# Two mab stages and a gated feed-forward on one Trainium2 core: earlier loads and transposes for the second batch, two dummy matmuls, one matmul fewer

## The chip, the cores and the metric

The kernel runs on one core of one Trainium2 chip. The core has a matrix engine (PE, with its weight loads shown apart as PEld), a vector engine (DVE), a scalar engine (ACT), a general engine (POOL) and a queue engine (SP). Each of them works through its own list of instructions in order; semaphores tie them together. DMA transfers are issued from the lists of SP and POOL and run beside them. The metric is the device time of one execution in microseconds.

## The reference

```python
def _attn_ref(x, inducing):                     # x: 4 x 12416 x 128, inducing: 32 x 128
    def mab(q, kv):
        s = scale * (q @ kv.transpose(0, 2, 1))
        s = s - s.max(-1, keepdims=True)
        a = np.exp(s)
        a /= a.sum(-1, keepdims=True) + 1e-09
        return a @ kv
    h = mab(I, x)                               # I: inducing for each of the 4 batches
    return mab(x, h)

def _moe_ref(x, w_gate, w_val, w_out):          # d_model 128, d_ff 1536
    gate = 1.0 / (1.0 + np.exp(-(x @ w_gate)))
    val = x @ w_val
    return gate * val @ w_out
```

For each batch, 32 inducing rows attend to all 12416 tokens and give `h` (stage 1). Every token then attends to the 32 rows of its batch's `h` (stage 2), and the result goes through a gated feed-forward.

## The kernel before, in words

A batch's 12416 tokens are 97 chunks of 128. They are handled in seven groups: six of 16 chunks and one of a single chunk (group 6). A group's tokens are loaded once into `xn` (`x_load`, issued from POOL's list) and are needed transposed in `xT`.

Stage 1 of a group: `s1_score` multiplies `xT` with the scaled inducing rows (L210) and DVE takes the negated maximum (`nm`, L222); `s1_exp` gives the exponentials `a1T` on ACT (L235); they are turned into `a1`, on PE with a copy (L248, L254) or by a DMA transpose (L259); `s1_sum` multiplies them with `xn` (L270). When all groups are through, their partial sums are brought to one maximum and added: that is `h` in transposed form, `hT`. Stage 2 of a group: scores of `xT` with `hT` (L443), maximum, exponential, sum and scaling, partly on POOL (L490 to L558). The attention weights `a2n` are turned by a DMA transpose from SP's list into `a2r` (L569).

The feed-forward doesn't use the attention output itself: `hw` holds the products of `h` with both weight matrices (L341), and 32 rows of `a2r` times 32 rows of `hw` give the two hidden halves at once (L850). The main loop runs over 97 blocks of four chunks; a block's 12 hidden chunks are eight steps `t`, alternately of two chunks and of one. A step is: `hidden_mm` for the value half and, two steps ahead, for the gate half on PE, tanh on ACT (`t`, L869), and the product `u = (t + 1) * v` on DVE (L882), which takes 776 steps with two of them cut in half. Two steps later `project` multiplies `u` with `w_out` on PE (L913).

Two steps are a slot. All other work of the loop is put beside the steps by a hand-written table: `at(slot, make)` records what is to be emitted behind the even step of a slot, or with `late=True` behind the odd one. What is emitted in a slot stands at that place in every engine's list, so a waiting instruction holds back what stands behind it on its engine. While the batch `b` is in the loop, the table holds stage 1 of batch `b + 1` (`plan_stage1`: score, exponential one slot later, turn two slots later, sums in the slots that are given) and stage 2 of both. `x_transpose_dma` issues one group's DMA transpose from `xn` to `xT` on SP (L90). PSUM tiles are named by tags; `m` is the one bank for all work of the table.

Before the loop stands a prologue for the first batch, for which nothing can be hidden: its groups are turned on PE (L637), and its last groups `sa`, `sb`, `sc` end with the chain that this change touches. The maxima of all groups are joined (`ml`, L708; L712, L713; `top`, L715), the weights `wl` are formed on ACT (L735), the four parts `hw_parts` are multiplied with them (POOL L737, ACT L738 and L748, DVE L750), and `h_add` adds them up by a matmul each (L756); `h_take` scales the sum to `hT` (L335). `keep_on(n, tag)` issues `n` matmuls of 128 x 512 whose result nobody reads (`w_ps`, L103).

Of the second batch's tokens two groups are loaded in the prologue and four in slot 3. Their transposes stand in the slots of this line, group by group:

```python
when = 3 * g if b else (9, 11, 14, 17, 20, 23, 12)[g]
```

Of the kernel before, what the change touches and what calls it, by code (L numbers as in the profile page):

```python
# [13 lines left out]
ALU = mybir.AluOpType  # L14
# [11 lines left out]
def kernel(  # L26
# [9 lines left out]
    nc = tc.nc  # L36
# [6 lines left out]
    NG = NCH // GC  # L43
# [29 lines left out]
    def x_load(b, s, first=0):  # L73
        c0, n = groups[s]
        if s == 0:
            c0, n = 0, n + NLO
        if b not in xn:
            xn[b] = xnp.tile([P, NCH, C], F16, tag="xn", name=f"xn_{b}")
        cuts = [c0, c0 + first, c0 + n] if first else [c0, c0 + n]
        for c, e in zip(cuts, cuts[1:]):  # L80
            nc.gpsimd.dma_start(xn[b][:, c:e, :], xv[b, :, c:e, :])  # L81
# [5 lines left out]
    def x_transpose_dma(b, s):  # L87
        c0, n = groups[s]
        xT_tile(b)
        nc.sync.dma_start(  # L90
            xT[b][:, c0 : c0 + n, :],
            xn[b][:, c0 : c0 + n, :].rearrange("p j c -> p (j c)"),
            transpose=True,
        )
# [5 lines left out]
    def keep_on(n, tag):  # L100
        w_ps = ps.tile([P, 4, P], F32, tag=tag, name="w_ps")
        for _ in range(n):
            nc.tensor.matmul(w_ps[:], idle[:, 0, :], idle, start=True, stop=True)  # L103
# [11 lines left out]
        out=identf[:],  # L115
# [18 lines left out]
        wo16[:].rearrange("p (q i) c -> p q (i c)", i=NI // 2),  # L134
        moe_w_out.rearrange("(q p i) c -> p q (i c)", p=P, i=NI // 2),
    )
    for g in range(2):
        x_load(1, g)

    ident = const.tile([P, P], F16, tag="ident")  # L140
# [42 lines left out]
    def s1_sum(b, s, a1, tag):  # L183
        hp = ps.tile([P, C + 1], F32, tag=tag, name="hp_ps")
        s1_sum_pe(b, s, a1, hp, 0, 4)
        return s1_sum_keep(b, s, hp)
# [3 lines left out]
    def at(slot, make, late=False):  # L190
        plan.setdefault((slot, late), []).append(make)
# [8 lines left out]
    def s1_dims(s):  # L200
        n = groups[s][1]
        ng = min(4, n)
        return ng, n // ng, 32 * ng
# [40 lines left out]
    def s1_turn_pe(b, s, a1T, tag="m"):  # L244
        ng, w, R = s1_dims(s)
        aT = ps.tile([P, 4, P], F16, tag=tag, name="aT_ps")
        for k in range(w):
            nc.tensor.transpose(aT[:, k, 0:R], a1T[0:R, ts(k, P)], ident[0:R, 0:R])  # L248
        return aT

    def s1_turn_copy(s, aT, copy=nc.vector.tensor_copy):
        ng, w, R = s1_dims(s)
        a1 = s1p.tile([P, 4, P], F16, tag="a1")
        copy(out=a1[:, 0:w, 0:R], in_=aT[:, 0:w, 0:R])  # L254
        return a1
# [31 lines left out]
    def plan_stage1(b, s, score, total):  # L287
        st = {}
        full = groups[s][1] == GC

        def begin():
            st["s1"] = s1_score(b, s, "m")

        def weigh():
            st["a1T"] = s1_exp(b, s, st["s1"])

        def turn():
            if full:
                st["a1"] = s1_turn_dma(b, s, st["a1T"])
            else:  # L300
                st["a1"] = s1_turn_copy(s, s1_turn_pe(b, s, st["a1T"]))

        at(score, begin)
        at(score + 1, weigh, late=full)
        at(score + 2, turn)
        first, second, keep = total

        def part(k0, k1):
            if k0 == 0:
                st["hp"] = ps.tile([P, C + 1], F32, tag="m", name="hp_ps")  # L310
            s1_sum_pe(b, s, st["a1"], st["hp"], k0, k1)

        at(first, lambda: part(0, 2))
        at(second, lambda: part(2, 4))
        at(keep, lambda: s1_sum_keep(b, s, st["hp"]))
# [12 lines left out]
    def l_inverse(l_ps):  # L328
        li = bp.tile([P, m], F32, tag="li")
        nc.vector.reciprocal(out=li[:], in_=l_ps)  # L330
        return li

    def h_take(b, h_ps, li):
        hT16[b] = bp.tile([P, m], F16, tag="hT", name="hT")
        nc.vector.tensor_tensor(out=hT16[b][:], in0=h_ps, in1=li[:], op=ALU.mult)  # L335
# [308 lines left out]
    a1T, a1 = {}, {}  # L644
    nm1, l1, hst = nm1s[0], l1s, hsts[0]
    for p in range(-2, NS - 3):
# [5 lines left out]
        if p >= 0:  # L652
            s = arrival[p]
            aT = s1_turn_pe(0, s, a1T[s])
# [5 lines left out]
        if p == EARLY - 2:  # L660
            we = const.tile([P, EARLY], F32, tag="we")
            nc.vector.tensor_reduce(
                out=nml[:, 0:1], in_=nm1[:, 0:EARLY], axis=AX.X, op=ALU.min
            )
            nc.scalar.activation(
                out=we[:], in_=nm1[:, 0:EARLY], func=AF.Exp, bias=nml[:, 0:1], scale=-1.0
# [19 lines left out]
    sc, sb, sa = arrival[-1], arrival[-2], arrival[-3]  # L686
# [4 lines left out]
    for j0, tag, copy in ((GC // 2, "v2", nc.scalar.copy), (GC - BC, "g1", nc.vector.tensor_copy)):  # L691
# [15 lines left out]
    ml = const.tile([P, 1], F32, tag="ml")  # L707
    nc.vector.tensor_reduce(out=ml[:], in_=nml[:], axis=AX.X, op=ALU.min)  # L708
    a1[sa] = s1_turn_copy(sa, s1_turn_pe(0, sa, a1T[sa]))
    low_ps = ps.tile([P, 2, 512], F32, tag="v2", name="low_ps")  # L710
    mlT_ps, arg_ps = low_ps[0:1, 0, 0:P], low_ps[:, 1, 0:NL]
    nc.tensor.matmul(arg_ps, identf[:], nml[:], start=True, stop=True, skip_group_check=True)  # L712
# [3 lines left out]
        out=top[:],  # L716
# [2 lines left out]
        op=ALU.min,  # L719
        negate=True,  # L720
    )
    a1[sb] = s1_turn_copy(sb, s1_turn_pe(0, sb, a1T[sb], "g2"), nc.scalar.copy)
    hps = [s1_sum(0, sa, a1[sa], "acc")]
    a1[sc] = s1_turn_copy(sc, s1_turn_pe(0, sc, a1T[sc], "v1"))
    for g in range(4):
# [8 lines left out]
    wl = const.tile([P, NL], F32, tag="wl")  # L734
    nc.scalar.activation(out=wl[:], in_=arg_ps, func=AF.Exp, scale=-1.0)  # L735
    hw_parts = [hpart[0][:]] + [hst[:, NS - k, 0:C] for k in range(1, NL)]
# [8 lines left out]
        out=e32l[:], in0=e32[:], scalar1=lsum[:], scalar2=TINY, op0=ALU.mult, op1=ALU.add  # L745
# [1 line left out]
    hps.append(s1_sum(0, sb, a1[sb], "m"))  # L747
    nc.scalar.mul(out=hw_parts[2], in_=hps[1], mul=wl[:, 2:3])  # L748
    hps.append(s1_sum(0, sc, a1[sc], "g1"))
    nc.vector.tensor_scalar_mul(out=hw_parts[3], in0=hps[2], scalar1=wl[:, 3:4])  # L750

    h_ps = ps.tile([P, m], F32, tag="g2", name="h_ps")
    l_ps = ps.tile([P, m], F32, tag="v2", name="l_ps")
# [1 line left out]
    def h_add(k, first=False, last=False):  # L755
        nc.tensor.matmul(h_ps[:], hw_parts[k], e32[:], start=first, stop=last)  # L756
# [1 line left out]
    h_add(1, first=True)  # L758
    nc.tensor.matmul(l_ps[:], ones[:], e32l[:], start=True, stop=True)
    h_add(0)  # L760
    h_add(2)
    h_add(3, last=True)
    h_take(0, h_ps[:], l_inverse(l_ps[:]))


    s2_a = ps.tile([P, GC, m], F32, tag="m", name="s2_ps")
# [4 lines left out]
        out=nmx_a[:], in_=s2_a[:, 0:BC, :], axis=AX.X, op=ALU.max, negate=True  # L771
# [3 lines left out]
        out=low[:],  # L775
        in0=s2_a[:, 0:BC, :],
        in1=nmx_a[:].unsqueeze(2).to_broadcast((P, BC, m)),
# [6 lines left out]
    for hf, tag in enumerate(("g1", "v1")):  # L784
# [7 lines left out]
        out=a2n_a[:],  # L792
        in0=e_a[:],
        in1=rs_a.unsqueeze(2).to_broadcast((P, BC, m)),
# [144 lines left out]
    for b in range(B):  # L939
        o = base[b]  # L940
        more = b + 1 < B

        if b == 0:
            plan_stage2(0, groups[1][0], o, None, o + 3, soon=True)
            plan_stage2(0, groups[2][0], o + 5, o + 7, o + 18)
        for s in range(3 if b == 0 else 2, NG - 1):
            k = o + 16 * s - 28
            plan_stage2(b, groups[s][0], k, k + 2, k + (14 if more else 10))
        plan_stage2(b, groups[NG - 1][0], o + 56, o + 58, o + 66, far=o + 52)
        if not more:  # L950
            continue
        early = (
            [(13, (18, 19, 19)), (16, (23, 23, 23))]
            if b == 0
            else [(8, (15, 16, 17)), (12, (18, 19, 19))]
        )
        later = [(24, (31, 31, 31)), (28, (35, 35, 35)), (40, (47, 48, 49)), (44, (50, 51, 51))]
        for s, (score, total) in enumerate(early + later + [(32, (43, 43, 43))]):
            plan_stage1(b + 1, s, o + score, [o + e for e in total])
        plan_combine(b + 1, o + 52, o + 55, [(o + 72, o + 74), (o + 80, o + 82)])  # L960
        plan_stage2(b + 1, groups[0][0], o + 67, o + 70, o + 78)
        plan_stage2(b + 1, groups[1][0], o + 84, o + 86, o + 94)
        for g in range(NS):
            when = 3 * g if b else (9, 11, 14, 17, 20, 23, 12)[g]
            at(o + when, lambda b=b, g=g: x_transpose_dma(b + 1, g))
            if b == 0 and 2 <= g < NG:
                at(o + 3, lambda g=g: x_load(1, g))
        if b + 2 < B:
            for g in range(NG):
                at(o + (28 if b == 0 else 24, 33, 42, 60, 60, 82)[g], lambda b=b, g=g: x_load(b + 2, g))  # L970
# [56 lines left out]
```

## Time and profile before

| what | value |
|---|---|
| time, median of 3 runs | 729.22 us (726.39, 729.22, 729.37) |
| the profiled execution's own time | 729.32 us |
| its span, first to last instruction | 727.5 us |
| mean granted clock of PE | 0.993 |
| first product `u` on DVE | 32.32 us from the span's start |
| HBM read and written | 27.80 MB and 25.43 MB |

All places in time are microseconds from the start of the span. In a row of the timeline stand the start, the duration (for several instructions from the first to the end of the last), the engine, the line, the operation with output and inputs, the count, and in brackets the engine's idle time ahead of it with what ended it. Rows of stretches give the busy time of each engine, with the number of instructions in brackets. The time of a run lies 1.82 us over the span of the profiled one.

### The profile page before, as it was taken

How to read it: one execution, taken by the hardware profiler on the slowest of the kernel's cores; microseconds unless marked ns; L12 is line 12 of the kernel's file. 1: busy time of each engine (PE TensorE's matmuls, PEld its weight loads, DVE VectorE, ACT ScalarE, POOL GpSimd, SP SyncE). 2: the span in 40 equal slices, each digit the busy share in tenths (PEclk: the TensorE clock that was granted, in tenths of full speed). 3: DMA queues.
4: the chain of work that ended last, by engine and by line, in shares of the span. 5: the costliest groups of instructions: out<-in, count | busy, mean ns of one | idle time of the engine just before them, and what ended most of it. 6: DMA issues, size and time to landing. Idle time of an engine off the chain costs nothing.

```text
span 727.5 us, 21568 instructions
## 1 busy us (share of the span) xinstructions
PE 649.0 (89%) x8478; PEld 392.9 (54%) x8478; DVE 704.4 (97%) x871; ACT 674.6 (93%) x1008; POOL 420.4 (58%) x699
## 2 busy tenths in 40 slices
PE   7888898999998988999988989999989899898887
PEld 4554555555555555555555545555555555555555
DVE  4798999999999999999999999999999999999998
ACT  4697999999999999999999999999999999999996
POOL 4471846788764548488757275387865665636200
PEclk9998999999999999999999999999999999999999
DMA  9797755154558272326188540330332121121211
GB/s 173 138 197 152 127 113 102 48 108 82 73 119 174 62 148 68 81 64 126 50 114 163 103 89 31 88 69 36 76 59 74 46 59 58 54 66 45 61 45 46
DMA packets 116726, 65.21 MB, mean 90 GB/s; under 512 B 99824, under 2 KB 101008, under 8 KB 116624
## 3 DMA queue, kind: packets, MB, share of 16 engines
q1 hardware_dynamic: 111936, 49.81, 31.1%
q0 software_dynamic: 4416, 13.90, 10.7%
q8 instruction: 66, 1.08, 0.6%
q14 instruction: 36, 0.29, 0.2%
q10 hardware_dynamic: 272, 0.13, 0.1%
HBM read 27.80 MB, written 25.43 MB: 73 GB/s over the span
## 4 chain that ended last, share of the span: by engine, by line
DVE 50%; issue 21%; PE 16%; ACT 9%; DMA 3%; DVEq 1%; POOL 0%; ACTq 0%; POOLq 0%
DVE u L882 48%; ACT t L869 8%; PE acc_ps L913 7%; PE v_ps L850 6%; DMA xn<-in_x_dram 2%; DVE nm L222 2%; DMA xT<-xn 1%; DVEq L882 1%; PE hp_ps L270 1%; PE g_ps L850 1%; POOL xn L81 0%; PE w_ps L103 0%; PE s_ps L443 0%; ACT hwt L351 0%; PE s_ps L210 0%
## 5 line engine op out<-in xcount | busy, mean ns | idle before, releaser
L882 DVE SCALAR_TENSOR_TENSOR u<-t,v_ps 128x512 f16<-128x512 f16 (+1 forms) x778 | 675.7, 945 | 3.8 <-PE g_ps L850 2.7
L869 ACT ACTIVATE t<-g_ps 128x512 f16<-128x512 f32 (+1 forms) x777 | 593.6, 818 | 32.3 <-ACT t L869 17.0
L850 PE MATMUL v_ps<-a2r,hwt 32*128 32x512 f16 (+1 forms) x1188 | 294.1, 372 | 65.3 <-DVE u L882 64.4
L913 PE MATMUL acc_ps<-wo,u 128*128 128x128 f16 x4656 | 329.0, 221 | 0.0
L913 PEld LDWEIGHTS <-u 128*128 128x128 f16 x4656 | 262.4, 98 | 89.2 <-issue 88.1
L850 PE MATMUL g_ps<-a2r,hwt 32*128 32x512 f16 (+1 forms) x1188 | 297.2, 379 | 0.0
L850 PEld LDWEIGHTS <-hwt 32*128 32x128 f16 x2424 | 91.0, 91 | 197.1 <-issue 152.2
L512 POOL TENSOR_TENSOR sum<-e 128x256 f32<-128x256 f16 (+1 forms) x23 | 15.5, 672 | 146.7 <-ACT e L504 145.2
L558 POOL TENSOR_TENSOR a2n<-e,rs 128x2048 f16<-128x2048 f16 (+3 forms) x25 | 86.8, 3475 | 5.6 <-DVE rs L530 2.4
L536 POOL TENSOR_TENSOR near<-sme,minus 128x16 f32<-128x16 f32 (+1 forms) x22 | 65.2, 2965 | 1.8
L931 ACT ACTIVATE o<-acc_ps 128x512 f32<-128x512 f32 x96 | 58.1, 605 | 0.0
L491 POOL TENSOR_SCALAR rise<-rise 128x256 f32<-128x256 f32 (+6 forms) x110 | 51.2, 466 | 9.7
L490 POOL TENSOR_TENSOR rise<-sc 128x256 f32<-128x256 f32 (+1 forms) x22 | 16.2, 738 | 38.6 <-ACT sc L480 38.4
L492 POOL TENSOR_TENSOR top<-top,rise 128x128 f32<-128x128 f32 (+3 forms) x88 | 28.4, 323 | 7.3
L512 POOL TENSOR_TENSOR sum<-sum 128x128 f32<-128x128 f32 (+3 forms) x92 | 28.4, 309 | 7.2
L490 POOL TENSOR_TENSOR rise<-top 128x128 f32<-128x128 f32 (+3 forms) x88 | 27.3, 311 | 6.9
L495 POOL TENSOR_TENSOR sc<-sc,top 128x512 f32<-128x512 f32 (+1 forms) x22 | 23.9, 1086 | 1.7
L443 PEld LDWEIGHTS <-xT 128*128 128x128 f16 x388 | 13.2, 96 | 11.7 <-issue 11.7
L443 PE MATMUL s_ps<-hT,xT 128*128 128x32 f16 x388 | 18.1, 178 | 0.3 <-DVE hT L335 0.3
L222 DVE TENSOR_REDUCE nm<-s_ps 128x1 f32<-128x512 f32 (+1 forms) x25 | 15.5, 618 | 2.3 <-PE s_ps L210 2.3
L235 ACT ACTIVATE a1T<-s_ps,nm 128x512 f16<-128x512 f32 (+1 forms) x25 | 15.7, 629 | 1.8 <-DVE nm L222 1.8
L492 POOL TENSOR_TENSOR top<-sc,rise 128x256 f32<-128x256 f32 (+1 forms) x22 | 16.2, 739 | 1.8
(132 smaller groups left out, 235.8 us busy)
## 6 DMA issues: line engine op xcount, KB each, us to landing
out_dram<-o SPq DMA_DIRECT2D x96, 256.0 KB, 2.3
xn<-in_x_dram POOLq DMA_DIRECT2D x19, 512.0 KB, 7.9
xn<-in_x_dram POOLq DMA_DIRECT2D x4, 544.0 KB, 5.7
a2r<-a2n SPq DMA_TRANSPOSE x29, 4.5
xn<-in_x_dram POOLq DMA_DIRECT2D x1, 384.0 KB, 14.8
wg<-in_moe_w_gate_dram POOLq DMA_DIRECT2D x1, 384.0 KB, 16.2
wv<-in_moe_w_val_dram POOLq DMA_DIRECT2D x1, 384.0 KB, 16.7
wo<-in_moe_w_out_dram POOLq DMA_DIRECT2D x1, 384.0 KB, 16.1
```

Source lines behind the costliest of these rows:

```text
L443: nc.tensor.matmul(s2[:, j, :], xT[b][:, c + j, :], hT16[b][:], start=(j == 0), stop=whole and j == j1 - 1, skip_group_check=True,)
L490: nc.gpsimd.tensor_tensor(out=r, in0=far, in1=near, op=ALU.subtract)
L491: nc.gpsimd.tensor_scalar_max(out=r, in0=r, scalar1=0.0)
L492: nc.gpsimd.tensor_tensor(out=top[:, 0:n, 0:w], in0=near, in1=r, op=ALU.add)
L512: nc.gpsimd.tensor_tensor(out=d[:, 0:n, :], in0=src[:, :, 0:w], in1=src[:, :, w : 2 * w], op=ALU.add)
L536: nc.gpsimd.tensor_tensor(out=near[:, 0:n], in0=sme[:, 0:n], in1=minus1[:, 0:n], op=ALU.pow)
L558: eng.tensor_tensor(out=a2n[:, 0:n, :, :], in0=e.unsqueeze(2).to_broadcast((P, n, 4, m)), in1=rs.unsqueeze(2).unsqueeze(3).to_broadcast((P ...
L850: st[what + "end"] = nc.tensor.matmul(pt[:, k, col : col + nb * P], hw[b][r : r + 32, j // 2, :], a2r[r : r + 32, o : o + nb, :].rearrange ...
L869: st["tanh"] = nc.scalar.activation(out=st["t"][:, :, c:e], in_=st["g"][:, :, c:e], func=AF.Tanh, scale=0.5)
L882: u = nc.vector.scalar_tensor_tensor(out=st["u"][:, :, c:e], in0=st["t"][:, :, c:e], scalar=1.0, in1=st["v"][:, :, c:e], op0=ALU.add, op1= ...
L913: nc.tensor.matmul(acc[0][(i // 2) % len(acc[0])][:, i, :], st["u"][:, k, ts(i, P)], wo16[:, NI * (j % 2) + j // 2, :], start=(j == 0 and ...
L931: nc.scalar.mul(out=o32[:], in_=acc[0][0][:], mul=0.5)
```

## The change

```diff
-    for g in range(2):
+    for g in range(3):
         x_load(1, g)
...
     a1[sa] = s1_turn_copy(sa, s1_turn_pe(0, sa, a1T[sa]))
+    aT = s1_turn_pe(0, sb, a1T[sb], "g2")
+    keep_on(1, "v1")
     low_ps = ps.tile([P, 2, 512], F32, tag="v2", name="low_ps")
...
-    a1[sb] = s1_turn_copy(sb, s1_turn_pe(0, sb, a1T[sb], "g2"), nc.scalar.copy)
+    a1[sb] = s1_turn_copy(sb, aT, nc.scalar.copy)
...
-    nc.vector.tensor_scalar_mul(out=hw_parts[3], in0=hps[2], scalar1=wl[:, 3:4])
+    nc.vector.scalar_tensor_tensor(
+        out=hw_parts[3],
+        in0=hps[2],
+        scalar=wl[:, 3:4],
+        in1=hw_parts[2],
+        op0=ALU.mult,
+        op1=ALU.add,
+    )
...
     h_add(0)
-    h_add(2)
     h_add(3, last=True)
     h_take(0, h_ps[:], l_inverse(l_ps[:]))
+    keep_on(1, "g1")
...
         early = (
-            [(13, (18, 19, 19)), (16, (23, 23, 23))]
+            [(9, (16, 17, 17)), (13, (23, 23, 23))]
             if b == 0
...
-            when = 3 * g if b else (9, 11, 14, 17, 20, 23, 12)[g]
+            when = 3 * g if b else (5, 7, 17, 19, 22, 25, 20)[g]
             at(o + when, lambda b=b, g=g: x_transpose_dma(b + 1, g))
-            if b == 0 and 2 <= g < NG:
-                at(o + 3, lambda g=g: x_load(1, g))
+            if b == 0 and 3 <= g < NG:
+                at(o + 12, lambda g=g: x_load(1, g))
```

Three groups of the second batch are loaded in the prologue and three in slot 12. The first two groups' transposes go to slots 5 and 7, the others to slots 17 to 25; the first two scores go to slots 9 and 13. In the prologue the transposes of `sb` are issued ahead of the joining of the maxima, with one dummy matmul behind them; the last part of `h` is multiplied and added to the one ahead of it in one DVE instruction, so that `h` takes three matmuls instead of four; and a second dummy matmul stands behind them.

On SP's list, in the first slots of the loop: before,

```order
L569 DMA_TRANSPOSE a2r<-a2n 128x8x128
L933 DMA out_dram<-o_856 128x512
L569 DMA_TRANSPOSE a2r<-a2n 128x16x128
L933 DMA out_dram<-o_1023 128x512
L90 DMA_TRANSPOSE xT_1036<-xn_113 128x16x128 x2
L90 DMA_TRANSPOSE xT_1036<-xn_113 128x1x128
L933 DMA out_dram<-o_1151 128x512
```

and with the change (`xn_113` and `xT` with four digits or 878 are the second batch's tiles, `o` a finished block):

```order
L569 DMA_TRANSPOSE a2r<-a2n 128x8x128
L942 DMA out_dram<-o_856 128x512
L90 DMA_TRANSPOSE xT_878<-xn_113 128x16x128 x2
L569 DMA_TRANSPOSE a2r<-a2n 128x16x128
L942 DMA out_dram<-o_1026 128x512
L259 DMA_TRANSPOSE a_1108<-a1T 128x4x128
L942 DMA out_dram<-o_1163 128x512
```

The two large transposes of `xT` stand ahead of the `a2r` transpose of blocks 4 to 7 and of the second output, and the small one is gone from here.

On PE's list, at the joining of the maxima in the prologue: before,

```order
L248 MATMUL aT_ps<-ident,a1T 128x128
L712 MATMUL low_ps<-nml,identf 128x4
L713 MATMUL low_ps<-identf,ml 1x128
L248 LDWEIGHTS a1T
L248 MATMUL aT_ps<-ident,a1T 128x128
```

and with the change:

```order
L248 LDWEIGHTS a1T
L248 MATMUL aT_ps<-ident,a1T 128x128
L103 LDWEIGHTS xT_87
L103 MATMUL w_ps<-xT_87 128x512
L714 MATMUL low_ps<-nml,identf 128x4
L715 MATMUL low_ps<-identf,ml 1x128
```

Eight transposes stand ahead of the joining instead of four, then the dummy.

At the end of the prologue's `h`, PE's list has before,

```order
L756 MATMUL h_ps<-e_124,hst_139 128x32
L759 MATMUL l_ps<-e32l,ones 128x32
L756 MATMUL h_ps<-e_124,hpart_313 128x32
L756 MATMUL h_ps<-e_124,hst_139 128x32 x2
L443 LDWEIGHTS xT_87
```

and with the change:

```order
L765 MATMUL h_ps<-e_125,hst_140 128x32
L768 MATMUL l_ps<-e32l,ones 128x32
L765 MATMUL h_ps<-e_125,hpart_314 128x32
L765 MATMUL h_ps<-e_125,hst_140 128x32
L103 LDWEIGHTS xT_87
L103 MATMUL w_ps<-xT_87 128x512
L443 LDWEIGHTS xT_87
```

One of the `h` matmuls is gone, and the dummy stands between them and the first scores of stage 2 (L443).

## The prediction, made before the changed kernel was run

> **What bounds the kernel now.** I read the page first, then the busy time by stretch, then the waits of VectorE (DVE), then the timeline at each wait.
>
> ```profile
> PE 649.0 (89%) x8478; PEld 392.9 (54%) x8478; DVE 704.4 (97%) x871; ACT 674.6 (93%) x1008; POOL 420.4 (58%) x699
> 0.00:32.00 32.00, 26.34 (x336) 15.13 (x337) 17.23 (x56) 15.90 (x35) 13.24 (x33) 0.95 0.90 172
> 32.00:60.00 28.00, 22.99 (x289) 13.58 (x288) 25.47 (x33) 24.12 (x36) 18.64 (x31) 0.97 0.89 167
> 60.00:70.00 10.00, 9.23 (x92) 5.52 (x90) 8.19 (x10) 7.97 (x12) 0.00 (x0) 0.74 0.54 121
> 70.00:120.00 50.00, 44.72 (x669) 27.45 (x667) 49.52 (x61) 48.20 (x76) 33.63 (x56) 1.00 0.60 118
> 120.00:200.00 80.00, 73.24 (x953) 44.71 (x953) 80.00 (x96) 77.50 (x117) 58.14 (x97) 1.00 0.44 82
> ```
>
> The columns behind each stretch are its length and the busy time of PE, PEld, DVE, ACT and POOL, then the granted clock, the DMA share and GB/s. From 120 us on DVE is never idle, and nothing in the diff takes work from it there. Its idle time, all that a reordering can win, is 14.77 us before 32 us, 2.53 up to 60 us, 1.81 up to 70 us, 0.48 up to 120 us. DVE's timeline places most of what lies behind 32 us:
>
> ```profile
> 49.48 8.17 DVE L882 SCALAR_TENSOR_TENSOR u<-t,v_ps 128x1024 f16<-128x1024 f16 x9
> 59.30 0.69 DVE L222 TENSOR_REDUCE nm<-s_ps 128x1 f32<-128x512 f32 x1 [1.65 <-PE s_ps L210]
> 61.78 1.82 DVE L882 SCALAR_TENSOR_TENSOR u<-t,v_ps 128x1024 f16<-128x1024 f16 x2 [1.20 <-PE g_ps L850]
> 64.14 3.11 DVE L882 SCALAR_TENSOR_TENSOR u<-t,v_ps 128x1024 f16<-128x1024 f16 x3 [0.54 <-PE g_ps L850]
> ...
> 52.35 7.47 SPq L90 DMA_TRANSPOSE xT<-xn  x3
> 58.63 0.62 PE L210 MATMUL s_ps<-xT,indT 128*32 128x512 f16 x4 [2.27 <-DMA xT<-xn]
> ...
> 52.35 6.24 DMA xT<-xn
> ```
>
> This is one event. The scores of the next batch's first group (slot 13) stand at the head of PE's queue at 58.63 - 2.27 = 56.36 us, but the transpose they read was issued only at 52.35 and landed 6.24 us later (last line, from the chain of waits). PE stood 2.27 us, and DVE behind it 1.65. Then PE ran at half clock and DVE lost 1.20 and 0.54 more. Granted clock by stretches of 3.4 us:
>
> ```profile
> 24.30:27.70 3.40, 3.02 (x74) 2.39 (x73) 2.01 (x8) 0.96 (x4) 0.60 (x1) 1.00 1.07 216
> 27.70:31.10 3.40, 3.40 (x32) 1.00 (x29) 2.27 (x10) 1.55 (x4) 0.41 (x2) 0.50 0.47 93
> 31.10:34.50 3.40, 2.93 (x38) 1.40 (x37) 2.29 (x5) 2.81 (x5) 1.46 (x3) 1.00 0.03 7
> ...
> 55.00:58.40 3.40, 1.37 (x18) 0.90 (x17) 2.65 (x3) 2.65 (x4) 2.37 (x6) 1.00 1.04 136
> 58.40:61.80 3.40, 3.17 (x24) 1.54 (x23) 1.30 (x3) 0.60 (x1) 0.00 (x0) 0.50 0.80 193
> 61.80:65.20 3.40, 3.40 (x28) 2.18 (x27) 2.86 (x3) 3.09 (x5) 0.00 (x0) 0.50 0.84 158
> ```
>
> The clock is 0.50 for exactly one such stretch (27.7 to 31.1, while the first hidden block is prepared) and for two behind the stall. So the stall costs 1.65 + 1.20 + 0.54 = 3.39 us in all.
>
> **Part 1, transposes, loads and scores.** The first transposes move from slots 9 and 11 to 5 and 7, ahead of the a2r transpose on SP's queue; the score moves from slot 13 to 9. A slot is two products, so four slots are eight of the nine products that run from 49.48 us for 8.17 us: about 8/9 of it, 7.3 us. The score will stand ready near 56.4 - 7.3 = 49.1 us (what the prologue gains moves it and the transposes alike). Can the data be there?
>
> ```profile
> 42.75 0.37 SPq L933 DMA_DIRECT2D out_dram<-o  x1
> 60.54 2.08 SPq L90 DMA_TRANSPOSE xT<-xn  x1
> DMA to landing us min/median/max: 4.4/4.4/4.4
> ...
> 49.29 1.94 SPq L569 DMA_TRANSPOSE a2r<-a2n  x1
> 36.94 2.23 POOL L81 DMA_DIRECT2D xn<-in_x_dram  x4
> 56.76 1.07 POOL L495 TENSOR_TENSOR sc<-sc,top 128x512 f32<-128x512 f32 x1
> 14.35 0.53 POOL L81 DMA_DIRECT2D xn<-in_x_dram  x1 [1.93 <-DMA xn<-in_x_dram]
> 17.74 0.20 POOL L669 TENSOR_TENSOR lwe<-l,we 128x4 f32<-128x4 f32 x1 [2.62 <-ACT we L665]
> ```
>
> SP comes free behind the first output at 43.1 us. The transpose issued at 60.54, with one output around it, took 4.4 us (the third line is its own). By that row the first group lands at 47.5 us, 1.6 us early. The slow bound is the stalled one's 6.24 us: 49.3 us, 0.2 late. Less is in flight ahead of it now than there, where an a2r transpose (49.29) and an output were: the four loads issued at 36.94 become three that stand on POOL behind the lowering of group 2, whose last step ends at 56.76 + 1.07 = 57.8 us. I take no wait, with 0 to 0.5 us as bounds.
>
> What is pushed back: the a2r transpose of blocks 4 to 7 (49.29) needs SP, and SP is done with both xT issues at 43.1 + 2 x 2.08 = 47.3 us, so a2r starts no later. If its data then moves behind the second xT's and takes the slow 6.24 us, it is there at 55.5 us; the first fill that reads it stands two slots behind the old score, at 56.4 + 3.6 = 60 us. Covered by 4.5 us; without that cover it would cost what it is late. The slot 12 loads serve scores from slot 28 on, fifteen slots after the old first score, as the third group is loaded early. Their issues (three quarters of 2.23, 1.7 us) lie where POOL had nothing (60 to 70 us: 0.00 busy).
>
> The third early load waits on POOL for an older one to land, as at 14.35 us (1.93 and 0.53 us), so until about 17.4 us. POOL's next real work, at 17.74, was itself waiting for ACT: 0 to 0.1 us. Its 512 KB move behind the weights, which come first in that queue, and DMA is idle from 31 us: 0.
>
> So part 1 gives back all 3.39 us (bounds 2.9 and 3.4).
>
> **Part 2, the prologue.** Its chain runs over PE:
>
> ```profile
> 22.16 0.40 PE L248 MATMUL aT_ps<-ident,a1T 128*128 128x128 f16 x4
> 22.81 0.38 PE L712 MATMUL low_ps<-nml,identf 128*128 128x4 f32 x2 [0.25 <-DVE nml L222]
> 23.44 0.40 PE L248 MATMUL aT_ps<-ident,a1T 128*128 128x128 f16 x4
> 31.78 0.82 PE L103 MATMUL w_ps<-xT 128*128 128x512 f16 x3
> 21.07 0.60 PE L103 MATMUL w_ps<-xT 128*128 128x512 f16 x2 [0.67 <-DVE xT L695]
> ...
> 25.21 0.36 ACT L748 ACTIVATE hst<-hp_ps,wl 128x128 f32<-128x128 f32 x1
> 25.56 0.35 DVE L750 TENSOR_SCALAR hst<-hp_ps,wl 128x128 f32<-128x128 f32 x1
> 26.08 0.39 PE L756 MATMUL h_ps<-e,hpart 128*128 128x32 f32 x2
> 26.31 0.61 PE L756 MATMUL h_ps<-e,hst 128*128 128x32 f32 x4
> 26.28 0.36 DVE L330 RECIPROCAL li<-l_ps 128x32 f32<-128x32 f32 x1 [0.38 <-PE l_ps L759]
> 26.95 0.19 DVE L335 TENSOR_TENSOR hT<-h_ps,li 128x32 f16<-128x32 f32 x1 [0.31 <-PE h_ps L756]
> ```
>
> The four transposes of 23.44 move into the gap of 0.25 us ahead of L712, with one dummy behind them. A dummy more costs 0.82 - 0.60 = 0.22 us, so PE is at most 0.03 us ahead there, and some 0.05 behind the later short waits: 0.05.
>
> One h matmul fewer takes 0.61 - 0.39 = 0.22 us off PE before hT. In exchange the last product adds the one from ACT and must wait for it (25.21 + 0.36 = 25.57): it starts at most 0.1 us later than 25.56, and its reader has slack, being behind h_add(0) at 26.08. The reciprocal ends at 26.64, so hT can't come before 26.68, 0.27 ahead. The dummy behind it sits in PE's wait for hT. I take 0.25 us for the two (bounds -0.3, if the dummy and the wait both fall on the chain, and 0.35).
>
> The clock between 27.7 and 31.1 is the unknown. The row shows 0.50 although PE was busy for 3.02 of the 3.40 us before it; the two dummies add streaming there. At full clock DVE's next reading is bounded by its own chain:
>
> ```profile
> 29.22 0.29 DVE L791 TENSOR_TENSOR a2n_a<-e_a,rs 128x128 f16<-128x128 f16 x1
> 30.05 0.62 PE L801 MATMUL a2T_ps<-ident,a2n_a 128*32 128x128 f16 x16
> ```
>
> a2n_a is done at 29.51 and PE could follow at once instead of at 30.05: 0.54 us. So 0 to 0.55; even odds, and I take 0.3.
>
> The Trainium skill, page "TensorE: Matmul & The Clock Gate", section "Part 1: The HAM clock gate", has a free-running window of 3.4 us that decides the clock, and half rate only after an idle window. The windows agree with the rows above; the idle window does not, as PE stood for 2.27 us of one and lost two. By the page's idle rule, with PE busy for 3.02 us, neither the drop at 27.7 nor a gain of the dummies would follow, and the sum would be 725.7 instead of 725.4, inside the forecast's own range below.
>
> **Sum.** The profiled run took 729.32 us, 1.82 over its span of 727.5, and stands 0.1 over the median of 729.22. 729.32 - 3.39 - 0.25 - 0.30 = 725.38 us, rounded to 725.4.
>
> **Rivals.**
> - The kernel has better runs than the profiled one: its lowest is 726.39, 2.93 less. That fits a stall without the half clock behind it (1.74) and more. From there the wait at 59.30 and part 2 are left to win: 726.39 - 1.65 - 0.25 = 724.5. For it: the windows run free, so what follows a gap is chance. Against: two of three runs were at 729.3.
> - A smaller wait at slot 9. If the transpose takes 7 us, PE stands 0.7 us longer than at 6.24, and the clock may drop behind it (1.74): 725.4 + 0.1 + 1.7 = 727.2. The slowest landing here (6.24) speaks against it.
> - The gain is given back: with DVE ahead, ACT (77.50 of 80.00 us) or PE sets the pace until 120 us and new gaps add 2 to 3 us: 728. Against it: DVE idles 0.48 us in the 50 us behind the stall.
> - Slower: the first transpose, its issue sharing SP with the second, lands so late that PE waits longer at slot 9 than it did at 13. Since the old wait of 2.27 us cost 3.39, this decides from a landing about 9 us after issue; at 9.5 us it costs 4.4 and gives 730.3. No row is near that.
>
> **How the numbers follow.** My forecast has 0.62, its own range 724.5 to 726.4; the better runs 0.18, the smaller wait 0.11, given back 0.05, slower 0.04. The line for faster by over 0.5% is 725.57, about what a measurement of this kernel can tell from no change, and my forecast lies close to it: a little over half of its weight is below. Faster 0.37 + 0.18 = 0.55, same 0.25 + 0.11 + 0.05 = 0.41, slower 0.04. The range takes in the better runs and the smaller wait: 723.9 to 727.6.
>
> **What would show it.** Right: no wait of PE for xT in slot 9, DVE idle in 32 to 70 us near 1 us instead of 4.34, a clock of 1.00 from 32 us on, hT 0.2 to 0.3 us earlier. Wrong: a wait of the scores for xT, a new half-clock stretch in the loop, or a first u that isn't earlier than 32.32 us.

## The result and the profile after

The changed kernel took 723.55 us (median of 6 runs, 723.41 to 723.66) against 728.82 us of the kernel before beside it (6 runs, 726.39 to 730.82): ratio 0.9929, 95% interval 0.991 to 0.9947. A second set of five runs gave 723.71 us and 0.9931 (0.9919 to 0.9943). The direction was forecast; the gain was larger than the 3.9 us of the sum, and the time lies 0.35 us under the range's lower end.

The profiled run took 723.41 us, its span is 721.6 us, 5.9 us shorter than before. Busy time by stretch, the columns as before:

```profile
0.00:32.00 32.00, 26.54 (x354) 15.42 (x354) 18.33 (x59) 17.33 (x38) 13.96 (x35) 1.00 0.98 188
32.00:60.00 28.00, 24.20 (x313) 14.38 (x310) 27.55 (x35) 26.27 (x38) 17.87 (x30) 1.00 0.64 120
60.00:70.00 10.00, 9.63 (x154) 6.17 (x153) 10.00 (x13) 9.74 (x16) 2.71 (x7) 1.00 1.13 191
70.00:120.00 50.00, 44.23 (x654) 26.94 (x650) 49.58 (x61) 47.78 (x74) 32.38 (x51) 1.00 0.74 136
```

DVE idles 0.45 us between 32 and 70 us, where it idled 4.34 before, and the granted clock is 1.00 in all four stretches. Before 32 us it is busy for 18.33 instead of 17.23 us, because the main loop begins earlier. The joining of the maxima (`ml`), the prologue's end and the new place of the first score, from the timeline, with the answer for the first transpose alone at the end:

```profile
22.71 0.16 DVE L708 TENSOR_REDUCE ml<-nml 128x1 f32<-128x4 f32 x1
26.03 0.38 PE L103 MATMUL w_ps<-xT 128*128 128x512 f16 x1
26.25 0.19 DVE L335 TENSOR_TENSOR hT<-h_ps,li 128x32 f16<-128x32 f32 x1
28.88 0.41 PE L810 MATMUL a2T_ps<-ident,a2n_a 128*32 128x128 f16 x16
30.83 0.69 DVE L891 SCALAR_TENSOR_TENSOR u<-t,v_ps 128x512 f16<-128x512 f16 x1 [0.66 <-ACT t L878]
...
41.58 6.63 SPq L90 DMA_TRANSPOSE xT<-xn  x2
47.74 0.40 PE L210 MATMUL s_ps<-xT,indT 128*32 128x512 f16 x4
49.01 0.68 DVE L222 TENSOR_REDUCE nm<-s_ps 128x1 f32<-128x512 f32 x1
...
L90 SPq DMA_TRANSPOSE xT<-xn x1: 3540/3540/3540, 41.6 to 41.6; - x1
DMA to landing us min/median/max: 6.1/6.1/6.1
```

No row here has a wait for xT: the scores at 47.74 us follow without a bracket, and DVE's maximum too. But the transpose landed at 41.58 + 6.1 = 47.7 us, at the very moment it was wanted.

Before, the same joining stood at 22.79 us:

```profile
22.79 0.16 DVE L708 TENSOR_REDUCE ml<-nml 128x1 f32<-128x4 f32 x1
```

The 5.9 us of the two profiled runs split so: hT comes 0.70 us earlier (26.95 to 26.25), the way from hT to the first product is 0.79 shorter (5.37 to 4.58), the wait at slot 13 with its two followers is gone (3.39), and so is the 0.26 us wait at 33.9 us. DVE's own work sums to 0.8 us less (704.4 to 703.6 on the two pages).

Of the 0.70 us, 0.62 is the change: the way from `ml` to hT takes 4.16 us before (22.79 to 26.95) and 3.54 now (22.71 to 26.25). The other 0.08 is an earlier start of the joining, which varies from run to run: in the second profile of the changed kernel `ml` starts at 23.10 and hT at 26.63. DVE's 0.8 us goes with the loop's edits: the eight profiles with the change's loop have 703.5 to 703.8 us, the four with the first scores in their old slots 704.2 to 704.4. How the edits shorten DVE's work, no run shows.

### The profile page after: what moved, and what is told of

It reads as the page before. It is cut to its first block, busy times and chain, and to the rows that moved or that the text cites. A ratio compares the mean times of both kernels' runs of the same rounds, so it can differ in the third digit from the quotient of the medians.

```text
span 721.6 us, 21567 instructions
## 1 busy us (share of the span) xinstructions
PE 645.2 (89%) x8478; PEld 390.9 (54%) x8478; DVE 703.6 (98%) x871; ACT 674.2 (93%) x1008; POOL 420.3 (58%) x699
## 4 chain that ended last, share of the span: by engine, by line
DVE 53%; issue 22%; PE 13%; ACT 8%; DMA 2%; DVEq 1%; POOL 0%; ACTq 0%; POOLq 0%
DVE u L891 51%; ACT t L878 7%; PE acc_ps L922 6%; PE v_ps L859 5%; DMA xn<-in_x_dram 2%; DVE nm L222 2%; DVEq L891 1%; PE hp_ps L270 1%; PE g_ps L859 0%; POOL xn L81 0%; PE s_ps L210 0%; ACT hwt L351 0%; PE s_ps L443 0%; PE aT_ps L248 0%; ACT a1T L235 0%
## 5 line engine op out<-in xcount | busy, mean ns | idle before, releaser
L490 POOL TENSOR_TENSOR rise<-sc 128x256 f32<-128x256 f32 (+1 forms) x22 | 16.2, 738 | 38.6 <-ACT sc L480 38.4
L443 PEld LDWEIGHTS <-xT 128*128 128x128 f16 x388 | 13.1, 96 | 11.7 <-issue 11.3
L81 POOL DMA_DIRECT2D xn<-in_x_dram x25 | 14.7, 595 | 6.3 <-DMA xn<-in_x_dram 5.5
L443 PE MATMUL s_ps<-hT,xT 128*128 128x32 f16 x388 | 18.1, 178 | 0.1
```

Source lines behind the costliest of these rows:

```text
L443: nc.tensor.matmul(s2[:, j, :], xT[b][:, c + j, :], hT16[b][:], start=(j == 0), stop=whole and j == j1 - 1, skip_group_check=True,)
L490: nc.gpsimd.tensor_tensor(out=r, in0=far, in1=near, op=ALU.subtract)
```

## The experiments

Each ran beside the kernel before, whose medians were 728.54, 728.55 and 728.7 us in the three sets. Where the time of single runs is given with a granted clock, that is the mean over a run's span.

**Only the loop.** The prologue is that of before but for the third early load; loads, transposes and scores are those of the change.

```diff
-    for g in range(2):
+    for g in range(3):
         x_load(1, g)
...
-            [(13, (18, 19, 19)), (16, (23, 23, 23))]
+            [(9, (16, 17, 17)), (13, (23, 23, 23))]
...
-            when = 3 * g if b else (9, 11, 14, 17, 20, 23, 12)[g]
+            when = 3 * g if b else (5, 7, 17, 19, 22, 25, 20)[g]
...
-            if b == 0 and 2 <= g < NG:
-                at(o + 3, lambda g=g: x_load(1, g))
+            if b == 0 and 3 <= g < NG:
+                at(o + 12, lambda g=g: x_load(1, g))
```

> The prologue of before with the new loads, transposes and score slots in the loop. Theory (the stall of 3.39 us goes, the prologue is worth another 1.5): no wait of PE for xT at slot 9, first u near 32.3 us, half clock from about 27.7 to 31.1 us, time near 725.2 us. Rival (the prologue's dummies also hold the clock in the loop, so that the loop's edits alone win little): 727 us or more, with a half-clock stretch behind 32 us.

Measured: 725.03 us (724.13 to 725.53), ratio 0.9945 (0.993 to 0.9961). No wait for xT at slot 9, as the theory has it. The time without the prologue's edits was not one but two: with a clock of 0.998 the runs took 724.88 to 725.40 us, with 0.999 or 1.0 724.13 and 724.23. The profiled one, 725.53 at 1.0, had a group of the first batch landing late (its transposes on PE start at 18.20 instead of 16.63 us), and the half clock expected near 28 us isn't in it: from hT to the first product it took 4.45 us, with the old prologue. So half clock comes in some runs and not in others, and costs about 1 us where it comes. That it lies in the prologue in the three runs at 0.998 wasn't seen, as none of them was profiled; in a run at 0.998 that was (four `h` matmuls, below) it does.

**Only the prologue.** The opposite: the change with the loop's four edits undone.

> The prologue of the change with the loop of before. Theory: first u near 30.8 us, full clock through the prologue, the wait of the scores at slot 13 back with about 3.4 us behind it, time near 727 us. Rival (an earlier prologue moves SP's transposes too, so the wait shrinks by itself): 725 us.

Measured: 727.68 us (12 runs, 726.78 to 730.38), ratio 0.9985 (0.9972 to 0.9998). Its timeline has the old wait, now 1.63 us for DVE:

```profile
30.95 0.69 DVE L891 SCALAR_TENSOR_TENSOR u<-t,v_ps 128x512 f16<-128x512 f16 x1 [0.65 <-ACT t L878]
57.36 0.40 PE L210 MATMUL s_ps<-xT,indT 128*32 128x512 f16 x4 [2.46 <-DMA xT<-xn]
57.80 0.69 DVE L222 TENSOR_REDUCE nm<-s_ps 128x1 f32<-128x512 f32 x1 [1.63 <-PE s_ps L210]
```

The first product is 1.37 us earlier than before, and the wait comes back as the theory said. What follows it is less: 0.32 and 0.55 us, so 2.50 in all instead of 3.39, with one stretch of half clock behind the wait instead of two. By medians the prologue alone wins 0.9 us, the loop alone 3.5, both 5.0 to 5.3.

**Early transposes against the old loads.** The change, with two groups loaded early and four in slot 3:

```diff
-    for g in range(3):
+    for g in range(2):
         x_load(1, g)
...
-            if b == 0 and 3 <= g < NG:
-                at(o + 12, lambda g=g: x_load(1, g))
+            if b == 0 and 2 <= g < NG:
+                at(o + 3, lambda g=g: x_load(1, g))
```

> The change with two groups loaded early and four in slot 3, as before; the transposes stay in slots 5 and 7. Theory (the first transpose is late because it shares the DMA engines with those loads): it is issued at 41.6 us as in the change but lands after 48 us, PE waits at slot 9 for 1 to 3 us, time 725 to 727 us. Rival (an early issue alone is enough): landing within 6.2 us, no wait, time 723.6 us.

Measured: 729.63 us (12 runs, 729.20 to 732.26), ratio 1.0015 (1.0002 to 1.0028): slower than before. The rival falls, and the theory was too mild.

```profile
41.72 11.44 SPq L90 DMA_TRANSPOSE xT<-xn  x2
52.78 0.62 PE L210 MATMUL s_ps<-xT,indT 128*32 128x512 f16 x4 [4.82 <-DMA xT<-xn]
53.45 0.69 DVE L222 TENSOR_REDUCE nm<-s_ps 128x1 f32<-128x512 f32 x1 [4.21 <-PE s_ps L210]
...
L90 SPq DMA_TRANSPOSE xT<-xn x1: 7916/7916/7916, 41.7 to 41.7; - x1
DMA to landing us min/median/max: 11.0/11.0/11.0
```

The same transpose, issued at the same place as in the change, takes 11.0 us instead of 6.1 with the loads beside it, and its issue alone holds SP for 7.9 us. PE stands 4.82 us at slot 9, and DVE loses 4.21, then 1.20 and 0.54 at half clock.

**Only the loads.** The kernel before with three groups loaded early and three in slot 12, and nothing else:

> The kernel before with only the loads moved: three groups early, three in slot 12; transposes in slots 9, 11 and on, scores in 13 and 16 as before. Theory (the loads in flight are most of what makes the transposes late): the first transpose, issued near 52 us, lands in 4.4 to 5.5 us, PE waits at slot 13 for 0.3 to 1.5 us and DVE for less than 1 us, no half clock behind it, time 725.5 to 726.5 us. Rival (its place on SP, behind an a2r transpose and an output, makes it late): the wait of about 2.3 us stays, 728.5 us.

Measured: 735.07 us (5 runs, 733.92 to 735.12), ratio 1.0085 (1.0071 to 1.0098). A clear miss, for two reasons that the profile shows:

```profile
52.01 7.78 SPq L90 DMA_TRANSPOSE xT<-xn  x3
58.70 0.57 PE L210 MATMUL s_ps<-xT,indT 128*32 128x512 f16 x4 [2.32 <-DMA xT<-xn]
61.34 9.75 SPq L90 DMA_TRANSPOSE xT<-xn  x1
71.20 1.21 SPq L259 DMA_TRANSPOSE a<-a1T  x1
73.70 0.30 PE L270 MATMUL hp_ps<-xn,a 128*32 128x128 f16 x4 [3.48 <-DMA a<-a1T]
74.78 0.69 DVE L882 SCALAR_TENSOR_TENSOR u<-t,v_ps 128x512 f16<-128x512 f16 x1 [3.28 <-PE g_ps L850]
```

The wait at slot 13 is as long as ever (2.32 us). The early loads have long landed and the next are issued only from 57.79 us on; the transpose, issued near 52 us behind an a2r transpose and an output and followed by a second one, takes 6.7 us. In the kernel before, too, the last of the four loads, issued at 38.6 us, had landed after 13.4 us, at 52.0, ahead of the transpose's issue at 52.35. So the old place was too late whatever the loads did. And the loads, now near 58 us, hit the transpose of slot 14: its issue holds SP for 9.75 us, the turn of the exponentials behind it (71.20) is late, and PE waits 3.48 us for that in a place where before it never waited.

**The scores' place.** The change with the first two scores and sums back in their old slots:

```diff
-            [(9, (16, 17, 17)), (13, (23, 23, 23))]
+            [(13, (18, 19, 19)), (16, (23, 23, 23))]
```

> The change with the first two scores in slots 13 and 16 and their sums as before; transposes and loads as changed. Theory (the turns of the exponentials must leave SP before the loads of slot 12 and the three transposes behind them fill the DMA engines): the second turn is stuck on SP behind the transposes issued from 64 us on, PE waits for it at slot 23, 1 to 4 us over the change: 724.5 to 727.5 us. Rival (the scores' place is free once the transposes are early): 723.6 us.

Measured: 732.01 us (11 runs, 729.05 to 739.68), ratio 1.0054 (1.0023 to 1.0085).

```profile
59.24 1.22 SPq L259 DMA_TRANSPOSE a<-a1T  x1
68.18 0.30 PE L270 MATMUL hp_ps<-xn,a 128*32 128x128 f16 x4 [3.27 <-DMA a<-a1T]
69.26 0.69 DVE L891 SCALAR_TENSOR_TENSOR u<-t,v_ps 128x512 f16<-128x512 f16 x1 [3.07 <-PE g_ps L859]
...
L259 SPq DMA_TRANSPOSE a<-a1T x1: 1224/1224/1224, 59.2 to 59.2; - x1
DMA to landing us min/median/max: 8.9/8.9/8.9
```

The wait is there, but at the first turn and not, as I had written, at the second, and not on SP's queue: it is issued in time at 59.24 us and takes 8.9 us beside the loads of slot 12. In the change that turn is issued at 52 us, ahead of them, and takes 2.4 us; the second, at 59.5, takes 8.3 us and has until slot 23. So the earlier scores are what makes slot 12 a place for the loads.

The three misplaced variants say one thing. Up to 80 us, a DMA transpose issued from SP with two or more bulk loads from POOL in flight took 7.5 to 11.9 us, one without any 2.4 to 6.7. The change has such transposes too (the first at 63.68 us takes 7.7), in a place where nothing waits for them. The Trainium skill, page "DMA: Bandwidth & Descriptors", section "Queues, rings and completion order", has each DMA engine go round-robin between the queues it has work for, packet by packet. The 6.1 against 11.0 us agree with a shared engine; that the packets alternate in this way, no trace here shows.

**The prologue piece by piece.** The order of the transposes undone:

```diff
-    aT = s1_turn_pe(0, sb, a1T[sb], "g2")
     keep_on(1, "v1")
...
-    a1[sb] = s1_turn_copy(sb, aT, nc.scalar.copy)
+    a1[sb] = s1_turn_copy(sb, s1_turn_pe(0, sb, a1T[sb], "g2"), nc.scalar.copy)
```

> The change with the transposes of sb back behind the joining of the maxima; dummies, three h matmuls and the loop as changed. Theory (the order of the transposes is worth some 0.4 us): 0.3 to 0.5 us over the change, near 723.95 us. Rival (the h matmul and the clock make all of the prologue's gain): 723.55 us.

Measured: 723.94 us (five runs at 723.90 to 723.99, one at 726.71). The sum of `h` by four matmuls (`h_add(2)` back, the last part multiplied alone):

> The change with h added up by four matmuls and the last part multiplied alone, as before. Theory: one more h matmul on PE's path is worth 0.2 us, near 723.75 us. Rival (the combined product on DVE waits for ACT and gives it back): 723.5 us.

Measured: 724.22 us; three runs at 723.79, 723.80 and 723.82, two with a clock of 0.998 and 0.997 at 724.62 and 726.20, and one at 725.44 with full clock. Against the 11 runs of the change (723.41 to 723.74, median 723.58) the order of the transposes is worth 0.35 us and the fourth matmul 0.22. Together that is the 0.6 us between the change and the two best runs of the loop alone. The traces say the same: from `ml` to hT it is 3.96 us with the transposes behind the joining and 3.74 with the fourth matmul, 0.42 and 0.20 over the 3.54 of the change.

**The dummies.** Both left out (`keep_on(1, "v1")` and `keep_on(1, "g1")`), only the one behind `h` left out, and the change itself once more:

> The change without its two new dummy matmuls. Theory (they hold the clock between hT and the first u): half clock for one stretch of 3.4 us in the prologue, hT to first u 5.3 instead of 4.6 us, time near 724.3 us. Rival (the shorter chain, not the dummies, keeps the clock; a dummy on PE only costs): clock stays at 1.00, time 723.3 to 723.5 us.

> The change without the dummy behind h, with the one behind the transposes of sb. Theory (the one behind h is what holds the clock between hT and the first u): some runs with one half-clock stretch, up to 1 us longer or more, the others at 723.5 us. Rival (the earlier dummy or the shorter chain holds it): all runs within 0.3 us of 723.55 us.

> The change itself once more. Theory (its two dummies and shorter chain hold the clock in nearly every run): all runs at 723.4 to 723.9 us, granted clock 0.999 or 1.0. Rival (the six clean runs were chance, since the clock's stretches run free): one or two runs in six with a clock of 0.998 or less, 1 to 3 us longer.

> The change without its two dummies once more. Theory (the dummies make the half clock rarer, not the runs without it shorter): clean runs at 723.5 us, and more runs with a half-clock stretch than the change beside it has. Rival (the dummies do nothing): as many as the change.

Measured: without both 723.95 us (723.46 to 726.42) and 724.30 (723.66 to 725.09); without the later one 724.54 (723.61 to 727.16); the change 723.71 (723.58 to 723.74). The profile of one run without both shows the half clock back, that of the change has none:

```profile
24.00:27.40 3.40, 3.00 (x76) 2.25 (x73) 2.23 (x9) 1.01 (x4) 0.60 (x1) 1.00 1.11 220
27.40:30.80 3.40, 3.19 (x38) 1.27 (x31) 2.46 (x9) 1.55 (x4) 0.61 (x3) 0.65 1.05 212
26.43 0.19 DVE L335 TENSOR_TENSOR hT<-h_ps,li 128x32 f16<-128x32 f32 x1
31.87 0.69 DVE L889 SCALAR_TENSOR_TENSOR u<-t,v_ps 128x512 f16<-128x512 f16 x1 [1.37 <-ACT t L876]
```

From hT to the first product it is 5.44 us here against 4.58 in the change: 0.86 us for one half-clock stretch, about what the kernel before lost. The first set without dummies had its profile in a run at full clock, with 4.59 us. But the profile with four `h` matmuls, which has both dummies, is of a run at 0.998 and shows the same stretch, with 5.36 us from hT to the first product:

```profile
24.00:27.40 3.40, 3.23 (x74) 2.44 (x75) 2.05 (x8) 0.99 (x4) 0.60 (x1) 1.00 1.12 222
28.00:29.00 1.00, 1.00 (x7) 0.36 (x4) 0.90 (x5) 0.85 (x3) 0.41 (x2) 0.50 1.04 209
26.61 0.19 DVE L335 TENSOR_TENSOR hT<-h_ps,li 128x32 f16<-128x32 f32 x1 [0.31 <-PE h_ps L758]
31.97 0.69 DVE L885 SCALAR_TENSOR_TENSOR u<-t,v_ps 128x512 f16<-128x512 f16 x1 [0.85 <-ACT t L872]
```

Counting runs with a clock of 0.998 or less: 0 of 11 with the change, 3 of 11 without both dummies, 4 of 6 without the later one, 3 of 6 with the old prologue; but also 1 of 6 and 2 of 6 in the two experiments above and 1 of 6 in the one below, which have both dummies. That is 4 of 29 with both dummies against 10 of 23 without (the versions that wait in the loop lose clock there in any case and are left out). The shortest runs without dummies (723.46, 723.65 and 723.66) are as long as the change's. So the dummies cost nothing that can be seen, and the counts speak for their making the half clock rarer; they don't rule it out, as the profile above shows, and which of the two does it is not shown.

**A version beyond the change.** The first two transposes stand in slot 4, ahead of the first output; the second group's sums and the third group's score each go one slot later:

```diff
-            [(9, (16, 17, 17)), (13, (23, 23, 23))]
+            [(9, (16, 17, 17)), (13, (24, 24, 24))]
...
-        later = [(24, (31, 31, 31)), (28, (35, 35, 35)), (40, (47, 48, 49)), (44, (50, 51, 51))]
+        later = [(25 if b == 0 else 24, (31, 31, 31)), (28, (35, 35, 35)), (40, (47, 48, 49)), (44, (50, 51, 51))]
...
-            when = 3 * g if b else (5, 7, 17, 19, 22, 25, 20)[g]
+            when = 3 * g if b else (4, 4, 17, 19, 22, 25, 20)[g]
```

> The change with its first two transposes in slot 4, ahead of the first output on SP, and the second group's sums in slot 24 and the third group's score in slot 25 (both one later, so that PE doesn't wait for the copy of the scores in slot 22). Theory: the first transpose lands near 43 us instead of 47.7, and DVE's idle time of 0.36 us at 75.6 us goes, near 723.2 us. Rival (the wait moves on to the next user of the bank): 723.5 us or more.

Measured: 723.10 us (six runs, four at 723.02 to 723.11, two at 724.10 and 725.73), ratio to the kernel before 0.9933 (0.9921 to 0.9945); the change beside it has 723.71. In its profile the transposes are issued from 36.16 us and land within 5.0, over 6 us ahead of the scores at 47.90, and DVE's products run without a gap from 69.4 to 78.2 us, where the change has 0.36 us of idle. That accounts for 0.36 of the 0.6 us; the rest was not taken apart, and neither were the earlier transposes and the later score. The first of the two transposes lands after 4.6 us here, with no output right ahead of it, where it takes 6.1 in the change.

## Why the prediction was right and where it was wrong

The direction and the size of the stall were right. The steps that failed are two terms of the sum, the prologue's chain to hT and the clock between hT and the first product: each was priced too low, 0.25 for 0.70 us and 0.30 for 0.79 between the two profiled runs. Against the forecast for the profiled run (725.38, measured 723.41) these two make 0.94 of the missing 1.97 us. The other 1.0 us was in no term: 0.26 for the wait at 33.9 us and 0.8 of DVE's own work, whose cause stays open.

- **What bounds the kernel.** Right in the main: 5.1 of the 5.9 us are idle time of DVE, nearly all of it before 70 us (DVE idles 727.5 - 704.4 = 23.1 us before and 721.6 - 703.6 = 18.0 after), and behind 120 us no idle time was won. The other 0.8 us is DVE's busy time, which I had taken as fixed.
- **The stall of 3.39 us.** Right in size: the loop alone wins 3.5 us by medians, and idle time between 32 and 70 us fell to 0.45, with near 1 us forecast. Part of it is half clock, which doesn't come in every run: between runs with a clock of 0.999 or 1.0 (726.27 to 726.47 before, 724.13 and 724.23 with the loop alone) it is 2.2 us. The rivals of a smaller wait, a gain given back and a slower kernel did not come.
- **Why it would go.** Partly wrong. I took the landing of 4.4 us from the transpose at 60.54, which had none behind it; the first of a pair right behind an output takes 6.1 to 6.7 us (change, loop alone, loads alone). The score found its data with nothing to spare, not 1.6 us early: that no wait followed is luck as much as foresight. And I put the old landing of 6.24 down to what was in flight ahead of it, the loads among it; those had landed at 52.0 us, ahead of its issue, and with the loads moved away it was 6.7. The loads matter in the other direction: left in slot 3 they would have made the early transpose land after 11.0 us, which is the slower rival's mechanism with the cause I had not priced.
- **The cover for what is pushed back.** The a2r transpose and the early third load cost nothing, as worked out, though the two issues held SP for 6.63 us and not 2 x 2.08, so that a2r was issued 0.46 us later, counted from the first product (17.43 against 16.97 us behind it), and not "no later". That the slot 12 loads cost nothing is right for the change, but rests on the scores having moved, which I had not seen as needed: in the old slots they cost some 8 us by medians.
- **The prologue up to hT.** Mis-sized: 0.25 us taken, upper bound 0.35; 0.70 in the profiles, of which 0.62 is the chain from `ml` to hT, and 0.6 by the experiments (0.35 + 0.22). The h matmul was right at 0.22. The transposes were not, with 0.05 taken and 0.35 to 0.42 measured: I set the dummy's 0.22 us against the gap of 0.25 and left out what the four transposes cost in their old place, between the joining and the weights. In the change's profile eight take 0.62 us and four took 0.40, so the second four add 0.22; the dummy starts at 22.55 and L714 behind it at 22.76, when its data comes anyway. With the transposes out of the way, everything behind the joining moves up.
- **The clock.** Mis-sized: 0.30 us taken with a bound of 0.55; 0.79 between the profiled runs, 0.86 between runs of the experiments. The bound was cut at the start of the a2T transposes. Up to there 0.47 us is won (from hT 3.10 us before, 2.63 now); the other 0.32 lies behind it. The transposes (0.62 to 0.41 us), the dummy and the first fills run at half clock too, and their gain was left out. That the profiled run had full clock there is in part luck: the counts above make it likelier with the dummies, not certain.
- **The rival of the better runs** gave 724.5 us from the run at 726.39. Its thought was right: the kernel before has a granted clock of 1.0 in three of the 34 runs of the first two sets (726.27 to 726.47) and 0.988 to 0.998 in the others (727.22 to 731.17), so much of its spread is half clock. The 11 runs of the change spread over 0.33 us, against 4.4 in the first six of the kernel before. That the spread is gone for good is not shown: of the 18 runs of the three other versions with its loop, or nearly, and both dummies, four had a clock of 0.997 or 0.998.
- **The clock rule.** The Trainium skill, page "TensorE: Matmul & The Clock Gate", section "Part 1: The HAM clock gate", says that the window runs free and does not start with the kernel. The runs agree: the same program has the half clock in some runs and not in others. Half rate only after an idle window, as it also says, does not: with four `h` matmuls PE was busy for 3.23 of the 3.40 us (24.0 to 27.4 us) right ahead of the half clock. Nor does PE's busy time tell the runs apart: without dummies, one run kept its clock with 3.00 of the same 3.40 us.

## What to carry to other kernels

Price the clock of a stage over the whole chain that runs in it, down to the first instruction of the bound engine, and not to the first place where another engine could take over. Before a DMA transpose or a bulk load is moved, list what else is on the DMA engines in both places: here the early transposes, the late loads and the early scores were each a loss alone or without the others, and a gain together. A transfer's landing is read from a row with the same neighbours on both sides, ahead and behind.

## What the runs showed of the hardware that was not expected

A DMA transpose of the same size landed after 4.4 us with none behind it (60.54, kernel before), 5.9 to 6.7 us as the first of a pair right behind an output, 4.6 us as the first of a pair with no output right ahead of it, and 7.5 to 11.9 us beside two or more loads from another queue. Its issue held SP's queue for 5.1 to 9.75 us beside loads instead of 1.8 to 3.7, so that everything behind it was late too. PE's clock was halved behind a stretch in which PE was busy for 3.23 of 3.4 us, in some runs of a program and not in others, and one such stretch between hT and the first product cost 0.8 to 0.9 us. Single runs 2 to 3 us longer than their set (726.42, 726.71, 726.20, 725.73, 727.16) have a clock of 0.990 to 0.998; where in the run that lies was not looked at, as no profile of one was taken.
